# A retention recurrence in steps of 64 tokens instead of chunks of 128, its burst in two parts

## The chip, the cores and the metric

The kernel runs on one core of a Trainium2 chip. The metric is the device time of one execution in microseconds (us). Before the change it is 1222.24 us, the median of 3 runs (1222.1 to 1222.4).

## The reference

Eight sequences of 576 tokens, eight heads of 64. For each head, with `gamma` of its own,

```
ret[i, j] = (q[i] . k[j]) / 8 * gamma ** (i - j)    for j <= i, else 0
attn      = ret @ v                                 # [8, 8, 576, 64]
x = attn, heads side by side                        # [4608, 512]
h = max(x @ w1, x @ w2, x @ w3);  z = h @ w_out     # 768 wide inside
g = (z @ u1) * (z @ u2) @ u3;     out = g @ u_out   # 1024 wide inside
```

All is float32 (the weights are given as float64). The change is in the first two lines, the retention.

## The kernel before

**Retention.** It is computed as a recurrence: within a chunk of tokens the scores are formed, masked and multiplied with v (own output); everything earlier comes in through one 64x64 state per head (state output); at the end of a chunk its sum of k and v (`gather`, here "sums") is added to the state and the state is scaled by gamma to the chunk's length (`update`). The powers of gamma that belong to single tokens are multiplied into q and v. A chunk has 128 tokens, or 64 at the end of a sequence and where a block of 512 tokens ends (`chunk_list`, L52): 40 chunks in all, 31 of them behind the opening.

On TensorE a float32 matmul of the retention shows as two MATMUL records, each with a weight load of its own. Scores are 16 matmuls of 64x64 by 128 columns for a chunk, taking the four quarters of the array in turn (L375); own outputs 8 of 128x64 (rows by columns of the array) by 128 columns (L390); state outputs 8 of 64x64 by 128 columns (L397); sums 8 of 128x64 by 64 columns (L410). Chunks of 64 tokens have 64 columns and fewer rows.

**Products.** The maxout's three matrix products are 12 matmuls of 128x128 by 512 columns for each of 18 (column tile, matrix) pairs and each of nine blocks of 512 tokens, in float32r, hi and lo parts (`products`, L484, matmul at L492); VectorE or ScalarE takes the maximum out of PSUM (`maximum`, L494) and the result is kept in DRAM (`keep`, L504).

**The order.** Two parts. The opening (the first two blocks of tokens) follows a list of names written out by hand (`ORDER`, L30). Everything behind it goes by a plan: `when(t, fn)` gives each step a due time in slots, one slot being one product of 12 matmuls (k = 18 * block + number), and the steps are issued sorted by due time. Each engine then works through its own queue in that order, and waits in it for what it needs. All loads and stores are issued by SyncE's queue (SP). Steps that `ORDER` calls "+" are taken from the plan.

Chunks behind the opening go in bursts of two (L469 to L479), at slots `t_o` that lie seven to eleven apart. Due times around a burst, with `t` the burst before it: q and k are fetched at t - 8 (the second chunk two slots later), scaled on GpSimd at t - 5, turned on VectorE by 32x32 blocks at t - 4.8 (L368); scores at t; masks at t + 0.6; v is scaled on GpSimd at t_o - 3.5; sums, own outputs, the first chunk's update and state output and then the second's all at t_o. The state output of the second chunk therefore waits for an update in the same burst.

```
        when(t, scores)
        when(t_o - 0.04, gather)
        when(t_o - 0.035 if slot == 0 else t_o + 0.5, update)
        when(t_o - 0.03, own_output)
        when(t_o - 0.01 if slot == 0 else t_o + 0.005, state_output)
```

PSUM has a ring of six banks (`ps_mm`) for products, scores and sums, and two banks for the outputs of a burst (`attn_ps`). Weights are converted from float64 words meanwhile: loaded into `raw` (six buffers) six slots ahead, then ScalarE (`words`, L172), VectorE (`scale`, L178, `join`, L181) and a store.

Of the kernel before, what the change touches and what calls it, by code (L numbers as in the profile page):

```python
# [9 lines left out]
F32 = mybir.dt.float32  # L10
F32R = mybir.dt.float32r
I32 = mybir.dt.int32
# [25 lines left out]
lo6 pr0.5 da6 ek8 db6 mx0.4 wo9 sl8 ou6 mx0.5 wo10 tq7 jn7 tq8 jn8 ft13 ga7 xh6 + sv8 eq7 pr0.6 hi7 xl6 hi8 lo7 lo8  # L38
eq8 pr0.7 mx0.6 up7 sl9 jn9 wo11 sc7 kp0.1 mx0.7 + hi9 sl10 sc8 pr0.8 + da7 wo12 db7 da8 db8 ou7 lo9 jn10 mx0.8 hi10
ga8 pr0.9 ft14 xh7 lo10 ft15 xl7 kp0.2 ft16 up8 ou8 mx0.9 + + + pr0.10 xh8 xl8 + pr1.0 mx0.10 sl11 jn11 wo13 pr1.2  # L40
sl12 ft17 mx1.0 sl13 hi11 wo14 lo11 pr1.6 sl14 wo15 jn12 wo16 jn13 pr1.3 jn14 mx1.6 hi12 hi13 lo12 hi14 pr1.1 lo13
mx1.3 lo14 sl15 jn15 wo17 pr0.11 mx1.1 hi15 mx1.2 lo15 kp1.0 sl16 pr1.5 mx0.11 jn16 kp0.3 sl17 hi16 pr1.4 lo16 jn17
hi17 pr1.9 mx1.4 mx1.5 lo17 kp1.1 pr0.12 mx1.9 pr1.7 mx0.12 + + + mx1.7 + + + + pr1.8 + + + + + + pr0.15 mx1.8 + + +
kp1.2 pr0.17 + + + + pr0.16 mx0.15 + mx0.16 + + mx0.17 kp0.5 + + + + + + + + pr0.14 + + + pr1.10 + + + + + + + +
pr0.13 mx1.10 pr1.12 mx0.13 + + mx0.14 + kp0.4 + + + + pr1.11 mx1.12 + + mx1.11 + + + kp1.3 + + + + + + + pr1.15 + + +
+ + + + + + + pr1.16 mx1.15 + + + + pr1.13 + + + + mx1.16 pr1.14 mx1.13 + + + + pr1.17 mx1.14 + kp1.4 + + + + + + +
mx1.17 + kp1.5 + + + + + + + + + + + + + + + + + + +
"""
# [17 lines left out]


def decay_tables():

    gamma = 1.0 - 2.0 ** (-5.0 - np.arange(H))  # L70
    i = np.arange(P)
    own = gamma.reshape(2, G)[i // D]
    qs = np.zeros((P, 2, 4, G))
    sd = np.zeros((P, 2, G))
    for j, c in enumerate((128, 64)):
        r = c // 32
        for e in range(r):
            qs[:, j, e] = own ** ((i % 32) * r + e)[:, None] / np.sqrt(D)
        sd[:, j] = own ** c
    vd = gamma[None, :] ** -i[:, None].astype(np.float64)  # L80
# [7 lines left out]
def tile_retention_maxout_bilinear(ctx: ExitStack, tc, a, out):  # L88
# [69 lines left out]
    def convert(t, loads, done, name=None):  # L158
# [95 lines left out]

    tables = cst.tile([P, 10 * G + H], F32, name="tables")
    qs = tables[:, :8 * G].rearrange("p (j T h) -> p j T h", j=2, T=4)
    sd = tables[:, 8 * G:10 * G].rearrange("p (j h) -> p j h", j=2)
    vd = tables[:, 10 * G:10 * G + H]
    turned = cst.tile([P, G, P], F32, name="turned")
    ident, mask = (cst.tile([P, P], F32, name=x) for x in ("ident", "mask"))  # L260

    rows = {}

    def below(dst, base, rows, op=ALU.is_ge):
        nc.gpsimd.affine_select(out=dst, in_=dst, compare_op=op, fill=0.0, base=base, pattern=[[1, P]], channel_multiplier=-rows)

# [11 lines left out]
    def make_mask():  # L278
        nc.gpsimd.memset(mask, 1.0)
        below(mask, 0, 1)  # L280

    def load_rows():
        rows["v"] = at.tile([P, G, P], F32, tag="qt", name="rows", bufs=4)[:2].rearrange("p h t -> p (h t)")
        load(rows["v"], a["rows"])

    def make_side():
        side = rows["side"] = at.tile([P, G, D], F32, tag="s", name="side")[:2, :2].rearrange("p h t -> p (h t)")
        nc.gpsimd.memset(side, 1.0)
# [17 lines left out]

    def attend(n, t=None, t_o=None, slot=0, pair=None):
        pair = {} if pair is None else pair
        b, t0, c, first, last = chunks[n]
# [7 lines left out]
        z = {}  # L317

        def fetch_qk():
            z["q"] = at.tile([P, 4, G, 32], F32, tag="q", name="q", bufs=3)  # L320
            z["k"] = at.tile([P, 4, G, 32], F32, tag="k", name="k", bufs=3)
            for x in "qk":
                for g in range(2):
                    for e in range(2):
                        o = D * g + 32 * e
                        load(z[x][o:o + 32, :r], a[x][b, G * g:G * g + G, t0:t0 + c, 32 * e:32 * e + 32].rearrange(
                            "h (t T) d -> t T h d", T=r))

        def fetch_kv():
            fetch_v()  # L330
            if not last:
                kn = at.tile([P, H, D], F32, tag="kn", name="kn", bufs=4)
                load(kn[:c], a["k"][b, :, t0:t0 + c, :].rearrange("h t d -> t h d"))
                z["kn"] = kn.rearrange("p (g h) d -> p g h d", g=2)

# [23 lines left out]

        def scale_q():  # L360
            nc.gpsimd.tensor_tensor(z["q"][:, :r], z["q"][:, :r], qs[:, j, :r].unsqueeze(3).to_broadcast([P, r, G, 32]), ALU.mult)  # L361

        def scale_v():
            nc.gpsimd.tensor_tensor(z["v"], z["v"], vd.unsqueeze(2).to_broadcast([P, H, D]), ALU.mult)  # L364

        def turn(x):
            z[x + "t"] = at.tile([P, G, P], F32, tag=x + "t", name=x + "t", bufs=2 + 2 * (x == "q"))
            nc.vector.transpose(out=z[x + "t"][:, :, :c].rearrange("p h (t T) -> p T h t", T=r), in_=z[x][:, :r])  # L368

# [42 lines left out]
        def update():  # L412
            s = z["st"]
            state[n] = at.tile([P, G, D], F32, tag="s", name="s")
            if not first:
# [13 lines left out]

        if t is None:  # L430
            steps = dict(fk=(fetch_pairs, "k", "kn"), fq=(fetch_pairs, "q", "q"), fv=(fetch_v,), tk=(swap, "k"), tq=(swap, "q"),
                         ek=(settle, "k"), eq=(settle, "q"), sc=(scores,), da=(decay, 0), db=(decay, 1), sv=(scale_v,),
                         ou=(output,), xh=(x_hi,), xl=(x_lo,))
            if not last:
                steps.update(ga=(gather,), up=(update,))
            for kind, step in steps.items():
                early(f"{kind}{n}", *step)
            return
# [6 lines left out]
        when(t, scores)  # L445
        when(t + 0.6 + 0.35 * lag, decay, 0)
        when(t + 0.9 + 0.35 * lag, decay, 1)
        if not last:
            when(t_o - 0.04, gather)
            when(t_o - 0.035 if slot == 0 else t_o + 0.5, update)  # L450
        when(t_o - 3.5 + 0.5 * lag, scale_v)
        when(t_o - 0.03, own_output)
        if not first:
            when(t_o - 0.01 if slot == 0 else t_o + 0.005, state_output)
        when(t_o + 0.5 + 0.25 * lag, x_hi)
        when(t_o + 1 + 0.25 * lag, x_lo)

    by_block = {}
    for n, (b, t0, *_) in enumerate(chunks):
        by_block.setdefault((b * S + t0) // N1, []).append(n)  # L460
    due = []
    for t, ns in by_block.items():
        for i, n in enumerate(ns):
            if t < EARLY:
                attend(n)
            else:

                due.append((n, t, T_BLK * (t - 1) - 0.52 + T_BLK * i / len(ns)))
# [5 lines left out]
    behind = bursts[0][0] - 9  # L474
    for t_o, some in bursts:
# [159 lines left out]
    with tc.manual_schedule():  # L635
        early("tables", load, tables, a["tables"])
        for name, step in (("warm", warm), ("rows", load_rows), ("side", make_side), ("ident", make_ident), ("mask", make_mask), ("wide", turn_rows)):
            early(name, step)
# [684 lines left out]
```

## Time and profile before

| | |
|---|---|
| median of 3 runs | 1222.24 us |
| profiled execution | 1223.12 us, its span 1221.4 us, granted clock 0.999 |
| opening, to the first scores of the plan | 0 to 103.6 us |
| recurrence and products | 103.6 to 493.8 us |
| products alone, then the later matrix products | 493.8 to 1221.4 us |

The span runs from the first to the last instruction. Matmuls overlap, so the length of one record is more than the distance from its start to the next one's start; the latter is what a train of matmuls costs. PEld is the weight load. "Idle before" is the engine's idle time ahead of an instruction, with what ended it.

### The profile page before, as it was taken

What the parts mean: (1) busy time and instruction counts of PE and PEld (TensorE: products, weight loads), DVE (VectorE), ACT (ScalarE), POOL (GpSimd) and SP (SyncE); (2) the same over time, 40 slices, a digit from 0 to 9 for tenths busy, and PEclk for the clock granted to TensorE, in tenths of its full rate; (3) what the DMA queues carried; (4) which work ended last, traced back from release to release, by engine and by line L of the source; (5) the groups of instructions that cost most, each with busy time, mean ns of one, the idle gap of its engine ahead of it and who ended that gap; (6) DMA issues with size and microseconds to landing.
All of it is one profiled execution on the core that took longest, in us unless ns stands there. A gap on an engine that the chain in (4) does not pass through costs nothing.

```text
span 1221.4 us, 22975 instructions
## 1 busy us (share of the span) xinstructions
PE 1208.2 (99%) x8900; PEld 1078.7 (88%) x8900; DVE 906.2 (74%) x1256; ACT 506.1 (41%) x873; POOL 311.9 (26%) x262
## 2 busy tenths in 40 slices
PE   8999999999999989999999999999999999999999
PEld 6888888888888878888889888888998888999998
DVE  5996677777877767366998467876666777998996
ACT  4651222233222322234556454443443344555554
POOL 2211221121211110000000125545244442344443
PEclk9999999999999999999999999999999999999999
DMA  9955788887998787444753733333333314455553
GB/s 219 252 127 121 161 204 230 196 213 180 223 221 172 168 172 192 146 128 165 227 185 122 251 112 130 129 121 119 107 115 136 128 59 159 155 165 166 176 169 104
DMA packets 323793, 199.34 MB, mean 163 GB/s; under 512 B 241634, under 2 KB 279266, under 8 KB 323684
## 3 DMA queue, kind: packets, MB, share of 16 engines
q1 hardware_dynamic: 323684, 197.87, 57.9%
q8 instruction: 70, 1.15, 0.4%
q14 instruction: 39, 0.32, 0.1%
HBM read 131.76 MB, written 66.06 MB: 162 GB/s over the span
## 4 chain that ended last, share of the span: by engine, by line
PE 88%; DVE 3%; DMA 3%; SPq 3%; issue 1%; POOL 1%; ACT 1%; DVEq 0%; POOLq 0%; ACTq 0%
PE ps_h L492 29%; PE ps_x L723 22%; PE ps_y L723 11%; PE ps_v L723 6%; PE ps_X L723 5%; PE ps_w L723 3%; SPq L99 3%; PE ps_Y L723 3%; PE o L390 2%; PE sc L375 2%; PE ps_V L723 1%; PE st L410 1%; PE o L397 1%; DMA q<-in_q_dram 1%; DMA raw<-in_moe_w_dram 1%
## 5 line engine op out<-in xcount | busy, mean ns | idle before, releaser
L492 PE MATMUL ps_h<-xh,w1h 128*128 128x512 f32 (+1 forms) x664 | 250.2, 378 | 0.0
L492 PE MATMUL ps_h<-xh,w1l 128*128 128x512 f32 (+1 forms) x664 | 247.4, 374 | 0.0
L492 PE MATMUL ps_h<-xl,w1h 128*128 128x512 f32 (+1 forms) x664 | 167.1, 374 | 0.0
L492 PEld LDWEIGHTS ps_h<-xh,w1h 128*128 128x128 f32 x664 | 125.5, 189 | 19.7 <-issue 2.1
L492 PEld LDWEIGHTS ps_h<-xh,w1l 128*128 128x128 f32 x664 | 125.6, 189 | 16.8 <-issue 0.3
L492 PEld LDWEIGHTS ps_h<-xl,w1h 128*128 128x128 f32 x664 | 123.7, 189 | 16.9
L1177 POOL TENSOR_TENSOR c<-c 128x512 f32<-128x512 f32 (+1 forms) x60 | 83.3, 1389 | 164.8 <-DVE c L1169 127.4
L502 DVE TENSOR_TENSOR hb<-ps_h,hb 128x512 f32<-128x512 f32 (+1 forms) x110 | 74.4, 677 | 62.8 <-PE ps_h L492 59.1
L1164 ACT ACTIVATE snap<-ps_x 128x512 f32<-128x512 f32 (+1 forms) x100 | 55.3, 554 | 151.4 <-PE ps_x L723 139.7
L361 POOL TENSOR_TENSOR q<-q,tables 128x512 f32<-128x512 f32 (+1 forms) x31 | 31.7, 1023 | 295.5 <-DMA q<-in_q_dram 224.9
L93 ACT ACTIVATE hb<-ps_h 128x512 f32<-128x512 f32 (+1 forms) x56 | 32.7, 584 | 173.7 <-PE ps_h L492 171.5
L172 ACT ACTIVATE e<-raw 128x512 f32<-128x512 f32 x64 | 54.1, 845 | 52.3 <-DMA raw<-in_moe_w_dram 35.4
L93 ACT ACTIVATE xh<-o 128x512 fp32r<-128x512 f32 (+1 forms) x40 | 22.1, 552 | 116.2 <-PE o L397 77.9
L368 DVE STREAM_TRANSPOSE qt<-q 128x512 f32<-128x512 f32 (+1 forms) x31 | 40.8, 1315 | 29.4 <-POOL q L361 29.4
L364 POOL TENSOR_TENSOR v<-v,tables 128x512 f32<-128x512 f32 x40 | 45.6, 1142 | 61.7 <-DMA v<-in_v_dram 44.4
L382 DVE TENSOR_TENSOR p<-sc,mask 128x512 f32<-128x512 f32 (+1 forms) x80 | 48.0, 627 | 11.2 <-PE sc L375 11.1
L178 DVE CUSTOM_DVE_ANT_0 m<-m,r 128x1024 uint16<-128x1024 uint16 x64 | 48.2, 753 | 6.9 <-ACT r L173 0.2
L96 POOL TENSOR_TENSOR ol<-raw,oh 128x512 fp32r<-128x512 f32 x1 | 1.3, 1265 | 203.7 <-DMA raw<-w3t_d 203.7
L173 ACT ACTIVATE r<-raw 128x512 int32<-128x512 uint32 x64 | 53.2, 831 | 0.0
L181 DVE SCALAR_TENSOR_TENSOR m<-raw,m 128x512 int32<-128x512 int32 x64 | 50.7, 796 | 0.2
L1169 DVE TENSOR_TENSOR c<-ps_x,snap 128x512 f32<-128x512 f32 (+1 forms) x40 | 25.1, 634 | 32.6 <-ACT snap L1164 13.3
L368 DVE STREAM_TRANSPOSE kt<-k 128x512 f32<-128x512 f32 (+1 forms) x31 | 41.0, 1324 | 8.7 <-DMA k<-in_k_dram 8.6
(302 smaller groups left out, 3257.9 us busy)
## 6 DMA issues: line engine op xcount, KB each, us to landing
zr<-g_d SPq DMA_DIRECT2D x18, 1024.0 KB, 6.1
raw<-in_moe_w_dram SPq DMA_DIRECT2D x34, 512.0 KB, 5.8
g_d<-c SPq DMA_DIRECT2D x64, 256.0 KB, 2.2
zr<-z_d SPq DMA_DIRECT2D x28, 512.0 KB, 6.5
h_d<-hb SPq DMA_DIRECT2D x54, 256.0 KB, 3.5
b<-h_d SPq DMA_DIRECT2D x16, 768.0 KB, 5.9
out_dram<-ob SPq DMA_DIRECT2D x35, 256.0 KB, 2.1
v<-in_v_dram SPq DMA_DIRECT2D x32, 256.0 KB, 4.7
```

Of the source, the lines that this page charges most:

```text
L93: nc.scalar.activation(dst, src, AF.Copy)
L172: nc.scalar.activation(z["e"], raw[:, :, 1].bitcast(F32), AF.Copy, scale=2.0 ** -112)
L173: nc.scalar.activation(z["r"], raw[:, :, 0].bitcast(U32), AF.Copy, scale=2.0 ** -29)
L178: nc.vector.tensor_tensor(z["m"], z["m"], z["r"], ALU.add)
L181: nc.vector.scalar_tensor_tensor(z["m"], z["hi"], -0x80000000, z["m"], ALU.bitwise_and, ALU.bitwise_or)
L368: nc.vector.transpose(out=z[x + "t"][:, :, :c].rearrange("p h (t T) -> p T h t", T=r), in_=z[x][:, :r])
L382: nc.vector.tensor_tensor(z[g][:c, :, :c], z["sc"][g][:c, :, :c], mask[:c, :c].unsqueeze(1).to_broadcast([c, G, c]), ALU.mult)
L492: nc.tensor.matmul(ps[:, cols], l, r, start=n == 0, stop=n == len(mms) - 1)
L502: nc.vector.tensor_tensor(hb, unwoven(ps[:, cols]), hb, ALU.max)
L723: nc.tensor.matmul(ps, l, r, start=start and j == 0, stop=stop and j == len(mms) - 1, skip_group_check=again)
L1164: nc.scalar.activation(t, unwoven(ps[:, :size]), AF.Copy)
L1177: nc.gpsimd.tensor_tensor(x, x, y, ALU.mult)
```

## The change

Behind the opening every step has 64 tokens. Two neighbouring steps (128 tokens, which may lie in two sequences) are handled together, two such pairs make a burst, and bursts lie nine slots apart: 28 pairs, 14 bursts. All retention matmuls of this part are 64x64 by 64 columns, in an order that takes the four quarters in turn. The burst has two parts: own outputs of one half and the next burst's sums two slots ahead of `t_o`; state outputs, the other half of the own outputs and the next burst's scores at `t_o`. The four updates are an addition on VectorE and a multiply on GpSimd each. The mask of two 64-token triangles takes the first half of `ident` (made in a new opening step `ends`); the `raw` buffers go from six to five, loaded five slots ahead; state buffers from two to eight. A ScalarE read of one column follows the first own outputs.

```diff
-            z["raw"] = cv.tile([P, 1024], I32, tag="raw", name="raw", bufs=6)
+            z["raw"] = cv.tile([P, 1024], I32, tag="raw", name="raw", bufs=5)
...
-            when(t - 6, fetch)
+            when(t - 5, fetch)
...
+    ends = [(0, 0), (1, 1), (0, 1), (1, 0)]
...
+    def attend(ns, t, t_o, t_sums):
...
+        def scores(slot):
+            z = zs[slot]
+            if slot == 0:
+                burst["sc"] = [bank("sc").rearrange("p (n h t) -> p n h t", n=2, h=G) for g in range(2)]
+            for h in range(G):
+                for g, s in ends:
+                    nc.tensor.matmul(burst["sc"][g][rows_of(s), slot, h], z["kt"][rows_of(g), h, rows_of(s)],
+                                     z["qt"][rows_of(g), h, rows_of(s)], start=True, stop=True)
...
+        def own_output(e):
...
+            for slot in range(len(ns)):
+                for r in range(2):
+                    for s in range(2):
+                        g = s ^ e
+                        for u in range(2):
+                            h = 2 * r + u
+                            nc.tensor.matmul(burst["o"][rows_of(u), g, slot, 2 * r + s], zs[slot]["v"][rows_of(s), G * g + h],
+                                             burst[g][rows_of(s), slot, h], start=e == 1 and slot == 0 and r == 0,
+                                             stop=slot + 1 == len(ns) and r == 1, skip_group_check=e == 0)
+            if e == 1:
+                nc.scalar.activation(turned[:, 0, :1], burst["o"][:, 0, len(ns) - 1, 3, :1], AF.Copy)
...
+        def update(slot, s):
...
+            else:
+                before = states[m]
+                nc.vector.tensor_tensor(new, x, before, ALU.add)
+                nc.gpsimd.tensor_tensor(new, new, ratio, ALU.mult)
...
+        for slot in range(len(ns)):
+            when(t_sums + 0.002, gather, slot)
+            when(t, scores, slot)
+            for s in range(2):
+                i = 2 * slot + s
+                when(max(t_sums + 0.5 + 0.45 * i, t + 0.5 if i == 3 else 0), update, slot, s)
+        when(t + 0.6, decay, 0)
+        when(t + 0.9, decay, 1)
+        when(t_o - 2, own_output, 1)
+        when(t_o - 0.03, state_output)
+        when(t_o - 0.02, own_output, 0)
...
         when(t - 8 + lag, fetch_qk)
-        when(t_o - 8.5 + 0.75 * lag, fetch_kv)
+        when(t_sums - 6.7 + 0.6 * lag, fetch_kv)
         when(t - 5 + lag, scale_q)
         when(t - 4.8 + lag, turn, "q")
         when(t - 4.7 + lag, turn, "k")
...
-        when(t_o - 3.5 + 0.5 * lag, scale_v)
+        when(t_sums - 2.6 + 0.5 * lag, scale_v)
...
     for t_o, some in bursts:
-        pair = {}
-        for slot, (n, _, _) in enumerate(some):
-            attend(n, behind, t_o, slot, pair)
-        behind = t_o
+        attend([n for n, _, _ in some], behind, t_o, sums)
+        behind, sums = t_o, t_o - 2
```

`state_output` and `gather` loop over the same four quarters, 16 matmuls for a pair where both of its steps read or leave a state.

## Rows read from the trace of the kernel before

**Rows 1.** The page's first part: busy time, share of the span, instructions of each engine.
```profile
PE 1208.2 (99%) x8900; PEld 1078.7 (88%) x8900; DVE 906.2 (74%) x1256; ACT 506.1 (41%) x873; POOL 311.9 (26%) x262
```

**Rows 2.** Windows, all engines: stretch, length, busy us (instructions), clock, DMA share, GB/s.
```profile
103.60:493.80 390.20, 385.16 (x3581) 336.54 (x3580) 284.22 (x426) 108.76 (x160) 66.91 (x72) 1.00 0.80 190
```

**Rows 3.** Windows, the products' line L492 alone (PE and PEld).
```profile
103.60:493.80 390.20, 307.51 (x1405) 263.99 (x1404) 1.00 0.80 190
```

**Rows 4.** The chain that ended last: start, us, what.
```profile
493.88 59.77 PE ps_h L492 x276
```

**Rows 5.** Timeline of TensorE, one burst: start, us, engine, line, out<-in, count.
```profile
236.89 1.03 PE L492 MATMUL ps_h<-xl,w1h 128*128 128x512 f32 x4
237.85 0.69 PE L410 MATMUL st<-v,kn 128*64 128x64 f32 x16
238.36 1.92 PE L390 MATMUL o<-p,v 128*64 128x128 f32 x32
240.21 0.67 PE L397 MATMUL o<-qt,s 64*64 64x128 f32 x16
240.70 1.93 PE L375 MATMUL sc<-qt,kt 64*64 64x128 f32 x64
242.56 0.48 PE L492 MATMUL ps_h<-xh,w1h 128*128 128x512 f32 x1
242.88 0.38 PE L492 MATMUL ps_h<-xh,w1l 128*128 128x512 f32 x1
```

**Rows 6.** Windows of the scores' line L375, then the own outputs' L390, alone.
```profile
103.60:493.80 390.20, 28.84 (x896) 26.37 (x896) 1.00 0.80 190
...
103.60:493.80 390.20, 28.36 (x496) 25.51 (x496) 1.00 0.80 190
```

**Rows 7.** Timeline of TensorE, starts of two bursts and two stalls.
```profile
337.82 1.15 PE L410 MATMUL st<-v,kn 128*64 128x64 f32 x32
...
438.26 0.68 PE L410 MATMUL st<-v,kn 64*64 64x64 f32 x16
...
440.80 0.69 PE L410 MATMUL st<-v,kn 128*64 128x64 f32 x16 [1.86 <-POOL v L364]
...
447.61 0.67 PE L397 MATMUL o<-qt,s 64*64 64x128 f32 x16 [1.27 <-DVE s L418]
```

**Rows 8.** Windows, all engines, the 20 us of the two stalls.
```profile
440.00:460.00 20.00, 17.93 (x183) 15.74 (x184) 16.03 (x26) 4.66 (x7) 3.03 (x3) 0.91 0.83 187
```

**Rows 9.** The state outputs' line L397 at 161.7: durations min/median/max, first and last start.
```profile
L397 PEld LDWEIGHTS o<-qt,s x16: 133/134/135, 161.7 to 161.9; 64*64 64x64 f32 x16
L397 PE MATMUL o<-qt,s x16: 216/218/218, 161.8 to 162.0; 64*64 64x64 f32 x16
```

**Rows 10.** Timeline of the same 16 matmuls and their weight loads.
```profile
161.67 0.38 PEld L397 LDWEIGHTS o<-qt,s 64*64 64x64 f32 x16
161.78 0.41 PE L397 MATMUL o<-qt,s 64*64 64x64 f32 x16
```

**Rows 11.** Groups by line and form, VectorE and GpSimd: busy, mean ns | idle before.
```profile
L382 DVE TENSOR_TENSOR p<-sc,mask 128x512 f32<-128x512 f32 x64 | 41.9, 682 | 11.2 <-PE sc L375 11.1
...
L368 DVE STREAM_TRANSPOSE qt<-q 128x512 f32<-128x512 f32 x25 | 37.7, 1506 | 27.5 <-POOL q L361 27.5
...
L416 DVE TENSOR_TENSOR s<-st,s 128x256 f32<-128x256 f32 x24 | 10.1, 420 | 11.3 <-PE st L410 7.2 <-PE o L397 4.1
...
L361 POOL TENSOR_TENSOR q<-q,tables 128x256 f32<-128x256 f32 x6 | 3.7, 618 | 45.5 <-DMA q<-in_q_dram 16.7 <-DVE xl L96 11.9 <-DVE m L177 9.3
```

**Rows 12.** Timeline of SP's queue, two of the fetches of q.
```profile
340.95 3.30 SPq L99 DMA_DIRECT2D q<-in_q_dram  x4
...
449.00 5.28 SPq L99 DMA_DIRECT2D q<-in_q_dram  x4
```

**Rows 13.** Timeline of SP's queue in the opening, weight loads 12 to 14.
```profile
52.61 3.24 SPq L99 DMA_DIRECT2D raw<-in_moe_w_dram  x3
```

**Rows 14.** Timeline of VectorE in the opening, the ninth join.
```profile
62.37 0.69 DVE L181 SCALAR_TENSOR_TENSOR m<-raw,m 128x512 int32<-128x512 int32 x1
```

More of the change, by code (lines that the diff above doesn't have):

```diff
@@ L65, in chunk_list, with pieces_of @@
     return out
+C = 64
+N_SUB, SUBS = NT // C, S // C
+def pieces_of(n):
+    subs = [divmod(2 * n + s, SUBS) for s in range(2)]
+    if subs[0][0] == subs[1][0]:
+        return [(subs[0][0], C * subs[0][1], P, 0)]
+    return [(b, C * j, C, C * s) for s, (b, j) in enumerate(subs)]
 def decay_tables():
@@ L72, in decay_tables @@
     own = gamma.reshape(2, G)[i // D]
[L73 to L80, printed above, removed]
+    qs = np.zeros((P, 4, G))
+    for e in range(4):
+        qs[:, e] = own ** ((i % 32 * 4 + e) % C)[:, None] / np.sqrt(D)
+    sd = np.stack([own ** c for c in (128, 64)], 1)
+    vd = np.stack([gamma[None, :] ** -(i % c)[:, None].astype(np.float64) for c in (128, 64)], 1)
     parts = (qs, sd, vd)
@@ L280, in make_mask, with make_mask2 @@
         below(mask, 0, 1)
+    def make_mask2():
+        nc.gpsimd.memset(mask2, 1.0)
+        below(mask2, C, 1)
+        below(mask2[:C], 0, 1)
     def load_rows():
@@ L305, in x_tiles, with attend_first @@
         return xs[t]
-    def attend(n, t=None, t_o=None, slot=0, pair=None):
-        pair = {} if pair is None else pair
+    def attend_first(n):
+        pair, slot = {}, 0
         b, t0, c, first, last = chunks[n]
@@ L317, in attend @@
         z = {}
[L319 to L334, printed above, removed]
         def fetch_v():
@@ L428, in x_lo @@
             low(nc.vector, parts(xl), z["o"][:, :, :, :c], parts(xh))
[L430 to L438, printed above, removed]
+        steps = dict(fk=(fetch_pairs, "k", "kn"), fq=(fetch_pairs, "q", "q"), fv=(fetch_v,), tk=(swap, "k"), tq=(swap, "q"),
+                     ek=(settle, "k"), eq=(settle, "q"), sc=(scores,), da=(decay, 0), db=(decay, 1), sv=(scale_v,),
+                     ou=(output,), xh=(x_hi,), xl=(x_lo,))
@@ new lines, in attend_first, with begins, closes, hand_over @@
+        if not last:
+            steps.update(ga=(gather,), up=(update,))
+        for kind, step in steps.items():
+            early(f"{kind}{n}", *step)
+    n_first = 0
+    while chunks[n_first][0] * S + chunks[n_first][1] < EARLY * N1:
+        attend_first(n_first)
+        n_first += 1
+    ends = [(0, 0), (1, 1), (0, 1), (1, 0)]
+    states = {}
+    def begins(m):
+        return m % SUBS == 0
+    def closes(m):
+        return m % SUBS == SUBS - 1
+    def hand_over():
+        states[EARLY * N1 // C] = state[n_first - 1]
@@ new lines, in feed, with fetch_qk, fetch_kv, scale_q @@
+    def feed(n, slot, z, burst, t, t_o, t_sums):
+        pieces = pieces_of(n)
+        blk, off = divmod(n * P, N1)
+        def fetch_qk():
+            z["q"] = at.tile([P, 4, G, 32], F32, tag="q", name="q", bufs=3)
+            z["k"] = at.tile([P, 4, G, 32], F32, tag="k", name="k", bufs=3)
+            for x in "qk":
+                for g in range(2):
+                    for e in range(2):
+                        for b, t0, c, at_ in pieces:
+                            o = D * g + 32 * e + at_ // 4
+                            load(z[x][o:o + c // 4], a[x][b, G * g:G * g + G, t0:t0 + c, 32 * e:32 * e + 32].rearrange(
+                                "h (t T) d -> t T h d", T=4))
+        def fetch_kv():
+            z["v"] = at.tile([P, H, D], F32, tag="v", name="v", bufs=4)
+            kn = at.tile([P, H, D], F32, tag="kn", name="kn", bufs=4)
+            for x, dst in (("v", z["v"]), ("k", kn)):
+                for b, t0, c, at_ in pieces:
+                    load(dst[at_:at_ + c], a[x][b, :, t0:t0 + c, :].rearrange("h t d -> t h d"))
+            z["kn"] = kn.rearrange("p (g h) d -> p g h d", g=2)
+        def scale_q():
+            nc.gpsimd.tensor_tensor(z["q"], z["q"], qs.unsqueeze(3).to_broadcast([P, 4, G, 32]), ALU.mult)
+        def scale_v():
+            nc.gpsimd.tensor_tensor(z["v"], z["v"], vd[:, 1].unsqueeze(2).to_broadcast([P, H, D]), ALU.mult)
+        def turn(x):
+            z[x + "t"] = at.tile([P, G, P], F32, tag=x + "t", name=x + "t", bufs=2 + 2 * (x == "q"))
+            nc.vector.transpose(out=z[x + "t"].rearrange("p h (t T) -> p T h t", T=4), in_=z[x])
+        def source():
+            return burst["o"][:, :, slot].rearrange("p g (r s) t -> p g r s t", s=2)
+        def parts(x):
+            return x[:, :, off:off + P].rearrange("p (g r) (s t) -> p g r s t", g=2, s=2)
+        def x_hi():
+            copy_r(parts(x_tiles(blk)[0]), source())
+        def x_lo():
+            xh, xl = x_tiles(blk)
+            low(nc.vector, parts(xl), source(), parts(xh))
@@ L444, in attend @@
         when(t - 4.7 + lag, turn, "k")
[L445 to L450, printed above, removed]
-        when(t_o - 3.5 + 0.5 * lag, scale_v)
-        when(t_o - 0.03, own_output)
-        if not first:
-            when(t_o - 0.01 if slot == 0 else t_o + 0.005, state_output)
+        when(t_sums - 2.6 + 0.5 * lag, scale_v)
         when(t_o + 0.5 + 0.25 * lag, x_hi)
         when(t_o + 1 + 0.25 * lag, x_lo)
-    by_block = {}
-    for n, (b, t0, *_) in enumerate(chunks):
-        by_block.setdefault((b * S + t0) // N1, []).append(n)
+    CHUNKS = N1 // P
     due = []
[L462 to L468, printed above, removed]
+    for n in range(EARLY * CHUNKS, NT // P):
+        t, i = divmod(n, CHUNKS)
+        due.append((n, t, T_BLK * (t - 1) - 0.52 + T_BLK * i / CHUNKS))
     bursts = []
@@ L474, in tile_retention_maxout_bilinear @@
     behind = bursts[0][0] - 9
+    sums = behind
+    when(behind, hand_over)
     for t_o, some in bursts:
-        pair = {}
-        for slot, (n, _, _) in enumerate(some):
-            attend(n, behind, t_o, slot, pair)
-        behind = t_o
+        attend([n for n, _, _ in some], behind, t_o, sums)
+        behind, sums = t_o, t_o - 2
     hbs = {}
```

83 lines of the change are left out of this document (60 added, 23 removed).

## The prediction

> **What bounds the kernel now.** The page comes first: TensorE is busy 99% of the span, VectorE 74%, and no other engine comes near [rows 1]. The windows by stage then fence off the part that the change touches: from the first scores behind the opening (103.6 us) to the last state product (493.8 us). There TensorE is busy 385.16 of 390.20 us, VectorE 284.22, ScalarE 108.76, GpSimd 66.91 [rows 2]. So a TensorE microsecond removed here is a microsecond of the kernel, unless something behind it comes late.
>
> The same window for the products' line alone counts 1405 matmuls [rows 3]. Behind the recurrence the same matmuls run undisturbed, 276 in 59.77 us, 0.2166 us each [rows 4]. 1405 x 0.2166 = 304.3 us, so the recurrence, its switches and its stalls hold 390.2 - 304.3 = 85.9 us. That is all that can be won.
>
> Where it goes is read from one undisturbed burst, start to start [rows 5]: sums 16 in 0.51 us (31.9 ns), own outputs 32 in 1.85 (57.8), state outputs 16 in 0.49 (30.6), scores 64 in 1.86 (29.1). Entering costs 0.10 (the product's fourth matmul starts at 236.89 + 3 x 0.216 = 237.54, the next was due at 237.75, the burst starts at 237.85); behind it the second product matmul starts 0.32 after the first instead of 0.216, again 0.10. With the counts of [rows 6] and of the plan (25 chunks read a state, 24 leave one, 16 records each): scores 896 x 29.1 ns = 26.1; own 496 x 57.8 = 28.7, less 2.8 for the 96 of 64 columns at half the price = 25.9; state 400 x 30.6 = 12.2, less 1.1 for 80 short ones = 11.1; sums 384 x 31.9 = 12.2; 16 bursts x 0.20 = 3.2. Together 78.5. The other 7.4 are stalls: 5.0 of TensorE idle [rows 2], the longest two 1.86 and 1.27 [rows 7], and the window 440 to 460 at a mean granted clock of 0.91, that is 3.6 us at 1.2 GHz behind the 1.86, which cost 1.8 [rows 8].
>
> **The change, part by part.** *Matmuls.* By the plan 28 pairs of steps give 448 score and 448 own-output matmuls; of the 56 steps 50 read a state and 49 leave one, eight matmuls each: 400 and 392. That is 1688, and the trace has two records for each such matmul: 3376. All are 64x64 by 64 columns, four in a row on four different quarters. The trace has that shape: 16 state products in 0.41 us, the last 0.22 of it one matmul's own length: 0.19/15 = 12.9 ns from start to start; their weight loads (0.38 - 0.134)/15 = 16.4 ns [rows 9, 10]. The upper bound is the same matmul of 128 columns, about 27 to 29 ns, if what paces a long train is not its columns. I take 14.0, near the matmul row and a little towards the weight loads, as a train of 100 lives less on loads made ahead than one of 16: 3376 x 14.0 = 47.3 us. (At 12.9: 43.6; at 16.4: 55.4; at 27.3: 92.2.)
>
> The Trainium skill (TensorE: Matmul & The Clock Gate, "Wait — 56ns, not 53.3ns?") speaks against this change: it says that start to start never falls under about 25 ns however few columns a matmul has. By that the 3376 would take 84.4 us. The 12.9 ns of [rows 9, 10] contradict it for four quarters in turn, over 16 matmuls; no row here shows a longer train.
>
> *Switches.* Each burst is now two visits: 28 instead of 16, and one ahead of the first. Every group has the same shape, so the switch between own and state outputs (0.10) goes; entry 0.10, leaving 0.11 (242.56 - 240.70 less 64 x 27.3 ns), the second matmul 0.10: 29 x 0.31 = 9.0. Inside a visit a change of group without a change of shape cost 0.06 (240.21 to 240.70, less 16 x 26.7 ns); 42 of them, 2.5.
>
> *Sum on TensorE:* 47.3 + 9.0 + 2.5 = 58.8 against 78.5: 19.7 us less.
>
> *State updates.* 49 steps instead of 24 chunks; each is an addition on VectorE (0.42) and a multiply on GpSimd (0.62 by its 128x256 row) [rows 11]. A chain of four with about 0.1 for each handover is 4.6 us. It is due from one and a half slots ahead of the scores, its result nine slots (over 23 us) later: hidden. Today's state wait of TensorE (1.27 in [rows 7], and shorter ones) goes with it. VectorE's queue stands while it waits for GpSimd, at most 3 x 0.8 us per burst; the maxima behind it have PSUM banks of a ring of six, and VectorE has a quarter of its time free. If that cover goes, it is 14 x 2.4 = 34 us of VectorE at the most, never all on TensorE.
>
> *VectorE otherwise.* By the plan 50 masks of 512 columns and 12 short ones become 28 of 512, at 0.68 each [rows 11] 15 us less and more with the short ones. Off the path, so nothing; it helps against the stalls. *Scaling of v* now stands ahead of the second pair's q on GpSimd, so the 1.86 us that the sums waited for v (its multiply stood behind a q that had not landed) should go. *ScalarE's* one-column read per burst, and the mask made in the opening, have no row; between 0 and 14 x 0.6 us on an engine that is 72% idle [rows 2]: nothing.
>
> *Loads.* SP's queue is second in line. (A slot of the plan is one product of 12 matmuls.) The first fetch of q behind slot 94 starts at 340.95, about when TensorE is there (burst of slot 93.48 at 337.82), the one planned at 123.48 at 449.00, when TensorE reached that slot at 438.26: SP falls 11 us behind [rows 7, 12]. VectorE waits in its queue for q, 27.5 us in all ahead of its turns [rows 11]. By either plan these slots hold 72 loads of q and k (one of the three pairs that lie in two sequences, whose loads are cut in two, is among them). TensorE will get through these 30 slots in 78 + 3.3 x 4.2 = 92 us where it took 100.4, so SP is later still. Hence I leave the stalls at 7.4 us: two old ones go, SP's lateness brings others.
>
> *Raw buffers 6 to 5.* Weight loads are planned one slot later, 2.6 us less lead. In the opening the 14th load must wait for the ninth join (62.37) instead of the eighth; SP passed it at about 55 [rows 13, 14]. So q and k of the first bursts start up to 7 us later, for scores at 103.6. Between 0 and 4 us; I take 1.
>
> **The sum:** 1223.12 - 19.7 + 1 = 1204.4 for an execution like the profiled one (span 1221.4 and 1.7 around it). The median of the runs shown lies 0.9 lower: 1203.5 us.
>
> **Rivals.** *A. Long trains do not keep the pace.* If the train is paced by issue, weight loads or instruction supply at the 27.3 ns of the 128-column scores, the matmuls take 92.2 instead of 47.3: 1248 us. It turns to slower from (78.5 - 11.5)/3376 = 19.8 ns on. For it: 64 columns leave two instructions 13 ns, and only trains of 16 are shown. Against it: both the matmuls and the loads of that train are well under 19.8. The skill's 25 ns would give 1241. Chance 0.13.
> *B. SP's queue takes part of it back.* The stretch from slot 94 to 124 keeps the 100.4 us that it has now, since the same loads come through one queue; 8.4 us are lost: 1212 us. For it: SP's lag, and the shorter lead of the raw loads, on which ScalarE waits in order. Against it: loads are issued eight slots ahead of use, and bursts come evenly every nine slots instead of seven to eleven. Chance 0.2.
> *C. The stalls go too.* States ready a burst ahead, v scaled early, VectorE over 15 us lighter: 7.4 less, 1196 us. Against it: SP's lag in [rows 12]. Chance 0.17.
> The forecast has the other 0.5, from 1199 to 1208.
>
> **How the numbers follow.** This kernel's runs tell 0.2%, 2.4 us, from no change. Faster by more: the forecast, B, C and a little of A's lower end, 0.84; slower 0.12; between them 0.04. Ten per cent left out below would be under C; above, most of A. Range 1193 to 1220.
>
> **What would show it.** Right: scores, own outputs and sums of the changed kernel at 13 to 16 ns from start to start in trains of 64 and more; 3376 records; two visits per nine products, each about 0.3 over its matmuls; no idle ahead of a state output; the stage from the first scores to the last state output some 20 us shorter; stages behind it unchanged. Wrong: weight loads at 20 ns or more (A), TensorE idle between slots 94 and 124 with VectorE waiting for q (B), or a first burst that starts later than 103.6.

## The result and the profile after

The changed kernel is 0.9% slower: 1234.94 us median (1229.2 to 1235.95, 5 runs) against 1222.4 us (1222.1 to 1225.7) for the kernel before in the same comparison, a ratio of 1.0086, 95% interval [1.0059, 1.0113]. The forecast was 1203.5 us. The profiled execution took 1233.12 us, its span 1231.1 us.

The recurrence itself became as cheap as forecast. The timeline of TensorE, a part of one burst of the changed kernel (start, us, engine, line, out<-in, count), against [rows 5]:
```profile
221.85 0.69 PE L480 MATMUL o<-p,v 64*64 64x64 f32 x32
222.36 1.11 PE L505 MATMUL st<-v,kn 64*64 64x64 f32 x64
...
228.78 1.16 PE L496 MATMUL o<-qt,s 64*64 64x64 f32 x64
229.76 0.65 PE L480 MATMUL o<-p,v 64*64 64x64 f32 x32
230.23 1.11 PE L462 MATMUL sc<-qt,kt 64*64 64x64 f32 x64
```
64 sums last 1.11 us; taking off the last one's own 0.22 leaves 0.89/63 = 14.1 ns from start to start, and the 64 scores show the same. The groups follow each other with the small gap that was forecast (222.36 - 221.85 = 0.51 us for 32 matmuls and one change of group).

Windows of the whole stage, from the first scores to the last visit of the recurrence, answering [rows 2] (length, busy us and instructions of PE, PEld, DVE, ACT, POOL, then clock, DMA share, GB/s):
```profile
105.27:501.60 396.33, 375.12 (x4782) 323.63 (x4782) 270.10 (x389) 106.07 (x171) 83.89 (x95) 0.98 0.79 186
```
TensorE is busy 10.04 us less than before (385.16), and yet the stage takes 6.1 us more: idle time went from 5.0 to 21.2 us. The granted clock fell from 1.00 to 0.98. The stage starts 1.7 us later, and what follows it takes 1.9 us more (729.5 against 727.6 us). Against the forecast, which had this stage 19.7 us shorter, nearly all of the loss to be explained is in the idle time and the clock of this stage.

What TensorE waited for in it (us in total, times, longest):
```profile
PE sc L462 <- DVE hb L630: 7.8, 4, 4.5
PE st L505 <- POOL v L563: 3.8, 3, 3.0
PE ps_h L620 <- DVE hb L630: 2.2, 2, 1.3
PE ps_h L620 <- ACT hb L103: 2.2, 2, 1.1
PE sc L462 <- issue: 1.9, 1, 1.9
PE sc L462 <- DVE kt L567: 1.8, 1, 1.8
PE ps_h L620 <- DVE s L519: 0.8, 1, 0.8
```
The same view one step further back, for the engines that TensorE waits on (`hb` are the maxima, `raw` the blocks of weights to convert, `kn` is the k that the sums read; rows of other waits left out at the dots):
```profile
POOL q L560 <- DMA q<-in_q_dram: 130.9, 23, 12.3
...
ACT e L182 <- DMA raw<-in_moe_w_dram: 103.2, 14, 15.0
...
DVE qt L567 <- POOL q L560: 49.1, 17, 5.3
...
POOL v L563 <- DMA v<-in_v_dram: 41.3, 12, 6.5
...
ACT e L182 <- DMA raw<-in_moe_w_out_dram: 19.3, 5, 7.7
...
DVE qt L567 <- DMA k<-in_k_dram: 15.4, 2, 9.4
DVE kt L567 <- DMA k<-in_k_dram: 11.9, 9, 3.5
```
VectorE waits 76.4 us for q and k ahead of its turns; before it was 38.0 (29.4 for GpSimd's q and 8.6 for k). Nearly all of these waits end at a load. Not everything that TensorE waited for does: 0.8 us are the new order's own (a product stood behind the addition of an update, L519), and for 2.5 us the trace names no wait ("issue", 1.9 and 0.6). The 2.2 us behind ScalarE's `hb` end at loads too: its queue stood 8.66 and 7.24 us for raw blocks just before them.

The longest stall shows the chain whole. TensorE, VectorE and SP's queue around 400 us, one fence each:
```profile
406.46 0.28 PE L462 MATMUL sc<-qt,kt 64*64 64x64 f32 x2
411.23 1.98 PE L462 MATMUL sc<-qt,kt 64*64 64x64 f32 x62 [4.50 <-DVE hb L630]
413.14 0.79 PE L620 MATMUL ps_h<-xh,w1h 128*128 128x512 f32 x1
```
```profile
404.60 1.20 DVE L567 STREAM_TRANSPOSE qt<-q 128x512 f32<-128x512 f32 x1 [9.38 <-DMA k<-in_k_dram]
...
409.58 1.08 DVE L567 STREAM_TRANSPOSE kt<-k 128x512 f32<-128x512 f32 x1 [2.70 <-DMA k<-in_k_dram]
410.51 0.67 DVE L630 TENSOR_TENSOR hb<-ps_h,hb 128x512 f32<-128x512 f32 x1
```
```profile
395.69 6.03 SPq L109 DMA_DIRECT2D q<-in_q_dram  x8
401.76 5.21 SPq L109 DMA_DIRECT2D k<-in_k_dram  x8
```
SP needs 5.21 us to issue the eight pieces of k of a pair that lies in two sequences and is done at 406.97; VectorE can turn k at 409.58; the maximum queued behind that turn frees a PSUM bank at 411.2; the scores had stood for that bank since 406.7. The scores wait for no load of their own; VectorE, which frees their bank, stands behind one.

From 409.9, still in the stall, the granted clock is 1.2 GHz, half of the full 2.4, for 6.8 us. Windows of 20 us, the second the same stretch as [rows 8]:
```profile
400.00:420.00 20.00, 15.50 (x208) 13.22 (x207) 10.94 (x19) 4.42 (x7) 2.28 (x3) 0.83 0.75 169
...
440.00:460.00 20.00, 17.62 (x215) 15.34 (x214) 17.42 (x28) 6.52 (x10) 4.89 (x6) 1.00 1.00 220
```
At 1.2 GHz it spent 17.1 us of the stage in four places (before: 3.4 us in one). 1.3 us of these lie inside the stall; half of the rest, 7.9 us, is what the low clock cost. The 440 to 460 stretch shows the other thing to watch: the mean share of the 16 DMA engines is 1.00, and TensorE idles 2.4 us at full clock.

### The profile page after: what moved, and what is told of

The parts are those of the page before. It is cut to its first block, busy times and chain, and to the rows that moved or that the text cites. A ratio compares the mean times of both kernels' runs of the same rounds, so it can differ in the third digit from the quotient of the medians.

```text
span 1231.1 us, 25359 instructions
## 1 busy us (share of the span) xinstructions
PE 1200.0 (97%) x10100; PEld 1066.5 (87%) x10100; DVE 893.3 (73%) x1220; ACT 504.8 (41%) x884; POOL 332.8 (27%) x290
## 2 busy tenths in 40 slices
DMA packets 326377, 200.13 MB, mean 163 GB/s; under 512 B 244210, under 2 KB 281842, under 8 KB 326260
## 5 line engine op out<-in xcount | busy, mean ns | idle before, releaser
L620 PE MATMUL ps_h<-xh,w1h 128*128 128x512 f32 (+1 forms) x664 | 254.7, 385 | 5.2 <-DVE hb L630 2.2
L620 PE MATMUL ps_h<-xh,w1l 128*128 128x512 f32 (+1 forms) x664 | 250.6, 379 | 0.7 <-DVE w1l L106 0.7
L567 DVE STREAM_TRANSPOSE qt<-q 128x512 f32<-128x512 f32 x28 | 42.2, 1508 | 65.0 <-POOL q L560 49.5
L560 POOL TENSOR_TENSOR q<-q,tables 128x512 f32<-128x512 f32 x28 | 29.4, 1051 | 158.8 <-DMA q<-in_q_dram 137.5
L520 POOL TENSOR_TENSOR s<-s,tables 128x256 f32<-128x256 f32 x43 | 28.7, 667 | 125.4 <-DVE s L519 125.4
L1297 DVE TENSOR_TENSOR c<-ps_x,snap 128x512 f32<-128x512 f32 (+1 forms) x40 | 25.1, 635 | 36.2 <-PE ps_x L851 17.1
L567 DVE STREAM_TRANSPOSE kt<-k 128x512 f32<-128x512 f32 x28 | 40.6, 1450 | 12.1 <-DMA k<-in_k_dram 11.9
L851 PE MATMUL ps_x<-t4h,a 128*128 128x512 f32 (+1 forms) x160 | 44.0, 359 | 0.3 <-DVE a L106 0.3
```

What stands on the lines that cost most here:

```text
L560: nc.gpsimd.tensor_tensor(z["q"], z["q"], qs.unsqueeze(3).to_broadcast([P, 4, G, 32]), ALU.mult)
L567: nc.vector.transpose(out=z[x + "t"].rearrange("p h (t T) -> p T h t", T=4), in_=z[x])
L620: nc.tensor.matmul(ps[:, cols], l, r, start=n == 0, stop=n == len(mms) - 1)
L851: nc.tensor.matmul(ps, l, r, start=start and j == 0, stop=stop and j == len(mms) - 1, skip_group_check=again)
```

## Experiments

All times are medians; a ratio is against runs of the kernel before on the same chip, with its 95% interval. What an edit gives over the changed kernel is the difference of the two ratios times 1222 us; the changed kernel's 1.0086 stands for all. With the intervals of both ratios such a difference is open by some 4 us either way.

**Is it the loads at all?** Three runs undo one part each.

*q and k loaded once.*
```
         def fetch_qk():
...
+            if once:
+                return
...
         def scale_q():
-            nc.gpsimd.tensor_tensor(z["q"], z["q"], qs.unsqueeze(3).to_broadcast([P, 4, G, 32]), ALU.mult)
+            z["q"] = at.tile([P, 4, G, 32], F32, tag="q", name="q", bufs=3)
+            z["k"] = once["k"]
+            nc.gpsimd.tensor_tensor(z["q"], once["q"], qs.unsqueeze(3).to_broadcast([P, 4, G, 32]), ALU.mult)
```


> The changed kernel, but q and k behind the opening are loaded once and every pair works on these same two tiles (the loads of q and k for the turned operands are left out, so the attention is not that of the inputs; all other instructions stay). Theory L (loads issued late by SP's queue hold VectorE, and so TensorE, and the clock falls behind each stall): products 304.5 + matmuls and switches 58.8 + opening 105.3 + tail 730 = about 1200, so 1198 to 1208 us. Rival U (the handover of each state update between VectorE and GpSimd holds the queues): 1225 or more. Rival R (five raw buffers and the shorter lead of the weight loads): 1222 or more, as the weight loads are unchanged.


1200.23 us, 0.9802 [0.9787, 0.9818]. Its stage, and all that TensorE waited for in it:
```profile
104.32:470.09 365.77, 364.29 (x4782) 316.73 (x4781) 271.33 (x389) 107.99 (x170) 84.44 (x95) 1.00 0.60 164
```
```profile
PE sc L463 <- issue: 1.5, 1, 1.5
```
With all 4782 matmuls of the changed kernel (3376 of the recurrence, 1406 of products) TensorE is busy 364.29 us, with 1.5 us idle at full clock. The loads of q and k hold the changed kernel, by 0.0284 x 1222 = 35 us; its matmuls don't.

*The update's multiply on VectorE* (`nc.gpsimd` to `nc.vector` in `update`).


> The changed kernel with the multiply of the state update on VectorE instead of GpSimd. U: VectorE no longer waits for GpSimd (13 waits, 8.5 us) and the queues free up, 1225 or less. L: VectorE has 43 x 0.42 us more of its own and is otherwise as late as before, 1232 to 1238.


1233.76 us, 1.0078 [1.0053, 1.0103]: the sharing with GpSimd costs nothing.

*The kernel before with five raw buffers*, lead 5.


> The kernel before with five raw buffers and the weight loads planned five slots ahead instead of six. R: most of the 12.5 us, 1230 or more. L: SP's order stays nearly as it was, 1221 to 1225.


1221.57 us, 0.9984 [0.9971, 0.9998]. Its first scores start at 105.11 instead of 103.61 us, so the opening does lose 1.5 us, but the total doesn't rise. Its stage will matter below:
```profile
105.11:491.55 386.44, 383.28 (x3582) 335.25 (x3581) 287.85 (x426) 107.47 (x160) 68.28 (x72) 1.00 0.82 192
```

**The pairs in two sequences.**
```
-                        for b, t0, c, at_ in pieces:
+                        for b, t0, c, at_ in [(pieces[0][0], min(pieces[0][1], S - P), P, 0)]:
```


> The changed kernel, but the three pairs that lie in two sequences load q and k in 8 pieces of 128 tokens instead of 16 of 64 (wrong tokens for half of each of these pairs). Theory L: SP's queue is 5.2 us shorter at three places, which hold TensorE idle for 1.8 and 4.5 us and at half clock behind it; 6 to 12 us less than the changed kernel, 1223 to 1229 us. U and R: 1233 to 1236, no difference.


1220.94 us, 0.997 [0.9959, 0.9981]: 24 issues fewer for the same bytes give 14 us, four tenths of the 35 and 2 us more than theory L's range allowed. Issued on ScalarE's queue (the second sequence's pieces alone):


> The changed kernel; of the three pairs in two sequences the second sequence's 8 pieces of q and k are issued by ScalarE's queue. Theory L (the time that SP's queue takes to issue, about 0.65 us a load): SP is relieved as in the run with uncut pairs, 1218 to 1224 us. Rival D (the DMA engines' own time, bytes and packets): the same transfers, 1231 to 1236.


1225.94 us, 1.0041 [1.0027, 1.0056], 5.5 us, between the two ranges. The kernel before cuts the same loads and bears it.

**Which way are they late?** Loads placed two slots earlier (`t - 10`):


> The changed kernel with q and k fetched ten slots ahead instead of eight. If what matters is the order in SP's queue (loads that VectorE waits for stand behind loads and stores that have time): 5.2 us more lead, 1212 to 1226. If SP is short of time in total, the lead is used up by the weight loads and it stays at 1229 to 1236.


1234.91 us, 1.0106 [1.0079, 1.0133]: nothing; v and kn behind them came late instead (TensorE's sums wait 9.4 us for GpSimd's v and 8.8 us for kn). All loads of k on ScalarE's queue:


> The changed kernel; every load of k for the turned operands (4 or 8 of the 8 or 16 of a pair) is issued by ScalarE's queue. L: SP is rid of 2.6 us per pair, 28 pairs, and ScalarE has the time (28% busy): 1203 to 1215 us. D: the same transfers, 1230 or more.


1230.36 us, 1.0078 [1.0059, 1.0097]. A miss for the theory that SP's issues are the limit: SP's rows add up to 263 us of the stage instead of 355 (the 360 of the expectations counts rows at the edges of windows twice). The share of the DMA engines rose to 0.83:
```profile
109.42:501.30 391.88, 375.35 (x4782) 324.23 (x4781) 264.07 (x389) 108.46 (x170) 84.94 (x95) 0.98 0.83 188
```
But ScalarE's in-order queue then waits 42 us for loads of k, so it isn't clean. The total also hides two changes: the first scores start 4.2 us later than in the changed kernel, and the stage itself is 4.5 us shorter.

*Thin loads*: as with q and k loaded once, but all loads issued, each with a quarter of its packets, into a tile that nobody reads.


> As the run with q and k loaded once, but all loads of q and k are issued as in the changed kernel, each with a quarter of its packets and bytes, into a tile that nobody reads (attention not that of the inputs). L with a fixed price per load: SP is as full as before but nobody waits for q and k; raw weights and v behind them are late: 1203 to 1215. D: a quarter of the bytes and no waits, 1199 to 1202.


1204.51 us, 0.9867 [0.9843, 0.9891], 27 of the 35 us; inside L's range and above D's.
```profile
105.11:472.60 367.49, 365.18 (x4782) 317.25 (x4781) 269.10 (x389) 108.14 (x170) 85.11 (x95) 1.00 0.66 173
```
These issues cost at most 8 us when nobody waits for what they bring; but a thin load takes SP 0.46 us instead of 0.67 to issue, and the run takes away DMA work too.

**A theory that fell: v's buffers.** SP's loads of v start right behind TensorE's visits, so I took v's four buffers for the gate of the queue.
```
-            z["v"] = at.tile([P, H, D], F32, tag="v", name="v", bufs=4)
+            z["v"] = at.tile([P, H, D], F32, tag="v", name="v", bufs=5)
...
-            z["k"] = at.tile([P, 4, G, 32], F32, tag="k", name="k", bufs=3)
+            z["k"] = at.tile([P, 4, G, 32], F32, tag="k", name="k", bufs=2)
```


> The changed kernel with v in five buffers instead of four behind the opening, and the turned k in two instead of three to make room; no load and no operation more or less. Theory V (SP's queue is held by v: the tiles live 17.7 slots of the schedule, almost two burst periods, so with four buffers each v load waits for TensorE's visit two bursts earlier, and the kn, q and k loads behind it in SP's queue come late): 1205 to 1215 us, the clock near 1.0 and SP's v loads no longer right behind the visit. Theory T (SP's queue is late because its issues, 0.67 us for each piece of q and k, and its waits for stores fill the stage, whatever buffer v has): 1229 to 1238 us, as the changed kernel.


1234.38 us, 1.0073 [1.0058, 1.0089]. With the straddling pieces on ScalarE's queue as well it took 1227.43, 1.0037 [1.002, 1.0053], where 1202 to 1211 was expected and 1226 without the buffers. And with v and kn fetched behind q and k:


> The changed kernel with the loads of v and kn of a burst placed behind those of its q and k (2.5 slots later for the first pair, 3.1 for the second), so that a v load that waits holds back no q or k of its own burst. Theory V: 1208 to 1220 us; v itself still lands in time. Theory T (the queue's issues fill the stage): no better than the changed kernel, 1228 to 1240 us, with GpSimd's multiply of v and TensorE's sums waiting for v and kn in place of VectorE for q and k.


1270.21 us, 1.0369 [1.034, 1.0398]: the sums then wait for v and kn (22.1 and 20.9 us), above the ranges of both theories. That v's loads start behind a visit does not show that they wait for it.

**Stores and turns.**
```
-            t += 2
+            t += 4
...
-                when(k + 2, keep, t, f)
+                when(k + (5 if t < n_blk - 1 else 2), keep, t, f)
```


> The changed kernel with the stores placed later in the order of the schedule, nothing else: h_d's three slots later and those of the converted weights two. In SP's queue, which is occupied 360 of the stage's 396 us, a store that waits for VectorE holds back the loads behind it. Theory S (a loop: loads come late, VectorE waits for them at its turns and at the words of the conversion, its maxima and joins come late, the stores wait for those, and SP's next loads wait behind the stores): 1208 to 1222 us, SP's rows of h_d and wp_d without waits. Theory T (SP is late by its own issues alone, about 263 us of the stage): 1228 to 1238 us.


1231.83 us, 1.0056 [1.004, 1.0073], 4 us, and not told apart from the changed kernel.
```
-        when(t - 5 + lag, scale_q)
-        when(t - 4.8 + lag, turn, "q")
-        when(t - 4.7 + lag, turn, "k")
+        when(t - 3.5 + lag, scale_q)
+        when(t - 3.3 + lag, turn, "q")
+        when(t - 3.2 + lag, turn, "k")
```


> The changed kernel with GpSimd's multiply of q and VectorE's two turns 1.5 slots later for each pair (some 4 us), the loads where they are: VectorE's queue then takes what waits for a load later. If the short time between load and turn is what makes VectorE late (theory P): 1210 to 1224 us, VectorE's waits for q and k, 76 us in the stage, mostly gone. Theory S: part of that, 1218 to 1230 us. If VectorE's waits at the turns aren't on the path: 1230 to 1240 us.


1229.3 us, 1.0039 [1.0022, 1.0056], 6 us. All that TensorE waited for in its stage:
```profile
PE st L505 <- DMA kn<-in_k_dram: 13.0, 5, 4.6
PE sc L462 <- DVE kt L567: 7.4, 5, 3.6
PE ps_h L620 <- issue: 1.1, 1, 1.1
PE ps_h L620 <- DVE hb L630: 0.3, 2, 0.2
```
The waits for a bank behind VectorE's turns, 10.0 us in the changed kernel, are down to 0.3, and yet TensorE idles 21.9 us as before: it now waits for kn, and for the turned k itself. VectorE's waits ahead of its turns did not go (76.5 us by the same view). Both:


> Both: stores later and turns later. Theories S and P together: 1201 to 1214 us, most of what loading q and k only once gave (1200.2 us) except the 24 more pieces of the straddling pairs. If neither is on the path: 1228 to 1240 us.


1226.6 us, 1.002 [1.0002, 1.0038]. 8 us together, a quarter of the loss: neither the loop through the stores nor the lead of the turns is the main cause.

**SP's issues or the DMA engines' work?**
Each raw load behind the opening brings a quarter:
```
+                if name is None:
+                    dst, src = (dst[:, :256], src[:, :256]) if len(dst.shape) == 2 else (dst[:, :4], src[:, :4])
```


> The changed kernel, in which each load of a raw weight block behind the opening brings a quarter of its bytes; the words that it leaves out are read from one small block loaded once, so the converted weights are wrong. ScalarE still waits for each load; SP issues as many loads as before (one more), and q, k, v and kn are untouched; the turned k has two buffers to make room. It takes some 15 MB out of the stage's 74 MB. Theory D (the 16 DMA engines, 0.79 busy over the stage and 0.9 to 1.1 in many of its 5 us windows, deliver late): 1203 to 1217 us. Theory T (SP's own issues) or S: 1226 to 1238 us, since no issue goes.


1217.66 us, 0.9938 [0.9914, 0.9962]: faster than the kernel before. It is 0.7 us above the range of theory D and 8 below that of T. The stage:
```profile
105.27:488.40 383.13, 370.70 (x4782) 321.42 (x4781) 273.83 (x389) 112.55 (x216) 86.05 (x95) 0.99 0.62 147
```
As many issues as in the changed kernel, 0.62 x 383.1 = 238 us of DMA time instead of 0.79 x 396.3 = 313, and 18 us less. What now waits for q, k and raw blocks (other rows left out at the dots):
```profile
ACT r L193 <- DMA raw<-in_moe_w_dram: 28.8, 10, 8.2
DVE qt L583 <- POOL q L576: 27.4, 11, 5.3
...
DVE qt L583 <- DMA k<-in_k_dram: 13.9, 2, 7.4
...
ACT r L193 <- DMA raw<-in_moe_w_out_dram: 9.4, 2, 5.7
DVE kt L583 <- DMA k<-in_k_dram: 7.4, 8, 2.5
```
VectorE's waits fell from 76.4 to 48.7 us (51.3 with one put down to a store) though no load of q or k was touched, ScalarE's for raw blocks from 122.5 to 38.2. The load of q itself is hardly quicker. Whole loads of q in the stage of the kernel before, of the changed one and of this run, count, KB, median us from issue to landing:
```profile
q<-in_q_dram SPq DMA_DIRECT2D x88, 64.0 KB, 3.5
...
q<-in_q_dram SPq DMA_DIRECT2D x88, 64.0 KB, 3.4
...
q<-in_q_dram SPq DMA_DIRECT2D x89, 64.0 KB, 3.2
```
So q and k come late because they are issued late, and not because the DMA engines take longer over each. SP's issues longer than 1 us add up to 57.9 us here and to 92.6 in the changed kernel, all shorter ones to 235 in both: what the lighter DMA load gave SP back is waiting, whether inside the issues or behind other engines.
The same loads, whole, on ScalarE's queue:
```
+            queue = nc.scalar if name is None else nc.sync
```


> The changed kernel with the loads of raw weight blocks behind the opening issued on ScalarE's queue; bytes and packets are the same. It takes some 90 issues and 60 us of occupation from SP's queue, 360 of 396 us. Theory T: 1208 to 1222 us. Theory D: 1228 to 1238 us, as the DMA engines have the same work.


1253.4 us, 1.0237 [1.0197, 1.0277], above both ranges. Taking some 90 issues off SP and leaving the DMA work costs another 18 us. Here too ScalarE holds its own work (waits of its x and hb behind loads, and TensorE's for v 14 us), so it speaks against moving, not for D alone. The Trainium skill says of this in "DMA: Bandwidth & Descriptors" (Rules for kernel authors) that spreading loads over queues brings no bandwidth, since all run on the same 16 engines. Both runs that moved whole streams agree (1230 and 1253 us); the one that moved 24 pieces gained 5.5 us. A saving of issue time is what the same rule grants.

**A version below both?**


> The changed kernel with stores and turns later, and the second sequence's pieces of the three straddling pairs issued on ScalarE's queue. Alone the three took 2.7, 5.4 and about 9 us off the changed kernel; if they add up: 1214 to 1222 us, below the kernel before. If the DMA engines' work alone sets what is left (theory D) the pieces bring nothing on top of later turns: 1223 to 1229 us.


1222.81 us, 0.9991 [0.9977, 1.0005], between the two ranges: 12 us off the changed kernel, where the three gave 15 singly (4 + 6 + 5.5). It is level with the kernel before, and no version of the changed kernel that loads all that it should is told to be faster.
```profile
104.10:489.26 385.16, 370.41 (x4782) 320.08 (x4781) 265.29 (x388) 107.73 (x170) 82.72 (x95) 0.99 0.81 191
```


> As that, with the q and k loads of a burst's two pairs four slots apart instead of two, the first pair's two slots earlier (v in five buffers, turned k in two, so that none waits for a buffer). The DMA engines' work is the same, but it comes in a lower crest. If the crest is what delivers late: 1206 to 1217 us. If the sum of the DMA work over the stage, or of the issues, is: no better than the run before it, 1214 to 1229 us.


1223.51 us, 0.9991 [0.9978, 1.0005]: a lower crest of loads brings nothing more.

## Why the prediction was wrong, step by step

*The matmuls:* right. 14.1 ns against 14.0 taken; 3376 records. Products and recurrence were forecast at 304.3 + 58.8 = 363.1 us of TensorE; where nothing was late it measured 364.29. Rival A is out. The Trainium skill's floor of about 25 ns ("TensorE: Matmul & The Clock Gate", "Wait — 56ns, not 53.3ns?") isn't what this trace shows for trains of 64 on four quarters in turn.

*Updates, the mask, ScalarE's read:* right to cost next to nothing (the multiply on VectorE changes nothing, and with q and k loaded once TensorE waits for none of them; in the changed kernel 0.8 us of its idle time stand behind an update). *Raw buffers:* 1 us was taken, the opening lost 1.5, within its bounds. *Scaling of v:* wrong. The 1.86 us that the sums waited for v were to go; they became 3.8 us in three waits, since v's multiply waited for the load of v itself (3.40 us ahead of the longest, 2.97, behind which the clock fell for 3.4 us).

*The loads: the step that failed.* "Hence I leave the stalls at 7.4 us: two old ones go, SP's lateness brings others." Those 7.4 us became 21.2 us of idle and 7.9 us lost to the low clock, 29.1 in all. The whole of the forecast gain went there: from 7.4 to 29.1 is 21.7 us, and 396.3 - (390.2 - 19.7) = 25.8 is what the stage lies above its sum; the 4.1 between the two stay unexplained. Some 4 of the 29.1 are no load's doing: the 2.5 us of "issue" and the 3.4 us of low clock behind the longer of its two stops.

Rival B had the direction, and in its own stretch the size: from the scores at slot 93.48 to those at 120.48 the changed kernel takes 91.8 us (349.55 to 441.39), with q and k loaded once 82.8 (332.55 to 415.35), so 9.0 us are lost there, where B had 8.4. But 16.1 us are lost ahead of that stretch and 5.5 behind it, where neither the forecast nor B looked. Nor did either see the way a late load spreads. In the longest stall it holds VectorE's queue at a turn, the maxima behind the turn hold PSUM banks, and TensorE stops at a bank rather than at the load; behind four of the stops the clock falls for 3.4 us or more. This way is not what makes the loss, though: with the turns later it was all but closed (10.0 to 0.3 us), and TensorE stopped as long, at kn and k.

A row that could have warned stood in [rows 2]: its DMA share, 0.80. 0.80 x 390.2 = 312 us of the 16 engines' time were in that stage before, and 313 are in it now, as the change takes no load away. In 370.5 us that asks for a share of 0.84 on average; 0.83 is the most that any run here reached over the stage, at 1230 us, and the two runs that came down to the forecast's stage had 0.60 and 0.66. A wall at 0.8 is not shown by this: the kernel before with five raw buffers had 0.82 with a full clock and 3.2 us of idle time, and windows of 5 us go above 1.2 in both kernels, as the share adds up the times of packets. SP's queue said the same: its issues, with their waits inside, add up to 349 of 390 us before (464 of them) and to 355 of 396 after (463). I read that queue in two places and took its lateness for something that the old plan bears, so the new would. So TensorE was one of three resources with little time to spare; shortening its work left the same loads less time, and they came late. Which of the other two gives way first is not shown.

*What is shown, and what stays open.* Shown: the loads of q and k, and not the recurrence, hold the changed kernel (35 us); the extra issues at the three straddling pairs are worth 5 to 14 of these; some 75 us of DMA work taken away without an issue are worth 18; the lead of the turns about 6. These overlap and were not all run together. Thin q and k loads cut as much DMA work (0.66 x 367.5 = 243 us are left) and give 27 us. Nobody waits for q and k there, and they take SP less time to issue; about 9 us hang on these two. Whether it is their place behind others in SP's queue or their own time to issue isn't settled: earlier, spread and moved loads didn't get it back. Nor is it told how much of the 18 comes by way of ScalarE and its raw blocks, or how DMA work makes SP late when the loads, once issued, land as soon as before.

## What to carry to other kernels

When the engine that bounds a stage is made faster, read the shares of the DMA engines and of the issuing queue for that stage, and divide the same load work by the shorter time before any gain is booked. A resource at 0.8 on average, with loads needed at set times, may not bear the shorter stage; this one bore 0.82 in the old order and did not reach 0.84 in the new. Ask of each late load not who reads it, but who stands behind its reader in the reader's queue and what that one holds; and when such a wait is taken away, look which load is the next to be late.

## What the runs showed of the hardware

Trains of 64x64 matmuls with 64 columns on four quarters in turn keep 14.1 ns from start to start over 64 of them. A load of q or k, 64 KB in 512 packets of 128 B, takes SP 0.67 us to issue; a half, 256 packets, takes nearly the same, 0.65, and a quarter, 128 packets, 0.46. In the DMA engines, 82,944 packets fewer (326,377 packets in the changed kernel, 243,433 with thin loads) took (313 - 243) x 16 = 1120 us of engine time away, an estimate of 14 ns each.

One kind of stall has no wait in the trace: TensorE stopped 0.6 to 2.7 us (once 4.1, in sums) with nothing named but "issue", mostly inside trains of scores, in the changed kernel twice and in 17 of the 20 runs at one place or another, but in neither run of the old order. The timeline of TensorE in the changed kernel:
```profile
258.93 1.11 PE L462 MATMUL sc<-qt,kt 64*64 64x64 f32 x63
261.97 0.21 PE L462 MATMUL sc<-qt,kt 64*64 64x64 f32 x1 [1.93 <-issue]
```
From 263.2 the granted clock is 1.2 GHz for 3.4 us, as it was from 136.9 with a stall of 2.97 us that ended at 136.58; and from 293.9 behind two short ones of 0.77 and 0.93 us. The trace has a likely cause: the instruction queue q8, which carried 79 packets of 16 KB instead of 70. Spread over TensorE's matmuls and weight loads (20,200, and 17,800 before) that is 64 bytes for each in both kernels, so q8 seems to bring TensorE's program. One packet starts at 259.56 and takes 0.94 us; the train goes on 1.5 us after its end. Of 34 such stops above 0.6 us in all runs, 33 end 1.2 to 1.7 us after the end of a q8 packet. That would mean that TensorE ran out of instructions there; no run tried it.
